# Column halves evicted from tiles of their own, weights loaded by K halves, attention rows dumped as they lie

## The chip, the core and the metric

The kernel runs on one core of one Trainium2 chip. A core has a matrix engine (TensorE; PE in the profile, with its weight loads shown as PEld), a vector engine (DVE), a scalar engine (ACT), GpSimd (POOL) and SyncE (SP), which here does nothing but issue transfers. Each engine works through its own list of instructions in order and waits on semaphores where it needs another engine's result. Sixteen DMA engines carry all transfers. A transfer that adds to what lies at its destination is issued by POOL; the plain ones are issued by SP, a few by ACT.

The metric is the device time of one execution in microseconds, the median of several runs.

## The reference

x has 2048 rows of 576 numbers in float32. The result is the sum of x, an attention and a two-layer network, both of the latter on the normalised rows.

```python
xn = _layernorm(x)
# attention: 32 heads of 18; each row looks at 8 rows: itself, 2 back, 4 back ... 14 back
qkv = (xn @ wqkv).reshape(B, S, 3, 32, 18)
idx = pos[:, None] - 2 * arange(8)[None, :]
logits = where(idx >= 0, einsum("bhsd,bhswd->bhsw", q, k[idx]) * 18 ** -0.5, -1e9)
A = einsum("bhsw,bhswd->bhsd", softmax(logits), v[idx]).reshape(B, S, 576) @ wo
# network: 576 -> 4608 -> 576
Bout = maximum(xn @ w1, 0) @ w2
out = x + A + Bout
```

## The kernel before, in words

**Precision.** Every operand of a matmul is split into a high and a low part in the type float32r, and three products (high times high, high times low, low times high) are added in PSUM. A split is two instructions, a copy on ACT (L172) and a subtraction on DVE (L176) or POOL (L174); `two` issues both.

**Stages.** The rows are cut into two phases of 1024 (even and odd rows). A phase has four blocks of 256 columns `tb` (each two row blocks of 128), and runs over the 36 blocks of 128 of the 4608 hidden columns. The first six blocks are multiplied plainly (`h_two`, `o_two`); the other thirty are taken in fifteen pairs p, two pairs of row blocks against two blocks of columns by Strassen's seven products. That makes 30 groups g in a phase; group g is for pair g // 2 of weights and pair g % 2 of `tb`. Each group is eight steps of TensorE, with places T and O in each step at which other work is issued. Between them run, for the four units u of eight heads, the qkv products; the attention itself (multiplications, reductions and softmax, all on DVE but the exponential) is a background list.

**What sets the order.** The program is written out in order by a planner: `on(ph, g, i, z, f, ...)` puts f at group g, step i, place T or O. The background list is issued by `run_bg`, which asks `room` how far DVE may run ahead of TensorE: up to the next of the due times DUE of a group (a step counts 1.46 us), 2.5 us at most. An instruction never moves at run time.

**Seeds.** A group keeps four banks of PSUM; `seed` (L977) opens bank q by copying bank a, and bank r by copying bank q, on ACT. The bank that is opened must have been read out before, by `relu_parts` (ACT L755, then DVE L759).

**Evictions.** The second matrix product leaves a block's 256 x 576 results in two PSUM tiles, columns 0 to 255 (h = 0) and 256 to 575 (h = 1). `evict` (L707) copies each half on ACT (L713) into one tile `ev` for both halves and both row blocks, of which there are two. When both halves are in, POOL issues two adding transfers to the output (L726), one for each row block, of 128 rows of 2304 bytes. In a group, the halves of one `tb` are evicted in steps 5 and 7, those of the other in steps 1 and 3 of the next group. The results of the output projection `wo` go out in the same way (L719), after the rows they add to have been added.

**Weights of the pairs.** `sw_load` (L894) brings four 256 x 128 pieces of w1 (two K halves for each of the two column blocks) in four transfers, and the 64 rows that are left over. `sw_mix` (L904) forms S1 to S4 of them on POOL (L909), `sw_prep` splits them.

**Attention rows.** `o_turn` turns a unit's result in blocks of 32 x 32 on DVE, `o_out` (L616) writes it to a DRAM tensor `od` in the order of the columns of the attention's result, by two transfers for each of four row groups r (L620 for 128 of the 144 columns, L624 for the other 16). When all units are there, `wo_rest` and `ot_in` bring the weights of `wo` and the rows of `od` back into SBUF (L257, L260; L395, L397), in five K tiles: four of 128 and one of 64, which is loaded twice.

## Time and profile before

| what | value |
|---|---|
| median of 3 runs | 1159.65 us (1159.57 to 1162.57) |
| profiled execution | 1158.69 us, span 1156.9 us, granted TensorE clock 0.994 |
| busy in the span: PE, DVE, ACT, POOL | 97%, 70%, 48%, 41% |
| DMA packets | 159811, 176.82 MB, 153 GB/s on average |
| adding transfers L726, POOL busy | 226.2 us |
| weight sums L909, POOL busy | 130.0 us, 120 of 1.1 us |
| subtractions L174, POOL busy | 95.8 us |
| seeds L977, ACT | 120 of 0.37 to 0.38 us |

Busy time counts what an engine executes, not what it waits for. A row of waits names the waiting engine, line and tile, then what released it, and the sum, number and longest of the waits. The chain of waits is followed back from the last instruction, so it shows what was late, not all that was slow. The time to landing of a transfer counts from its issue. PE's busy time comes near the whole span because matmuls overlap; the stalls have to be looked for in the waits.

### The profile page before, as it was taken

The page shows a single profiled execution, that of the slowest core. Times are in us where ns is not written, and L with a number is a line of the kernel's source. Part 1 is how long each engine was busy: PE and PEld are TensorE (multiplying, and loading weights), DVE is VectorE, ACT ScalarE, POOL GpSimd, SP SyncE. Part 2 cuts the span into 40 slices and gives each one's busy share as a digit, 9 for nine tenths or more (in the row PEclk, how much of TensorE's full clock was granted, in tenths as well). Part 3 has the DMA queues.
Part 4 walks back from the last instruction along what each step waited for, and adds up shares of the span by engine and source line. Part 5 has one row for each costly group of instructions (what it writes and reads, how often), then busy time and mean ns, then how long its engine had stood idle before and what let it go on. Part 6 is the DMA issues. An engine that isn't in the chain of part 4 may idle for free.

```text
span 1156.9 us, 38381 instructions
## 1 busy us (share of the span) xinstructions
PE 1116.8 (97%) x16410; PEld 1094.4 (95%) x16410; DVE 814.3 (70%) x1249; ACT 560.3 (48%) x1348; POOL 469.5 (41%) x514
## 2 busy tenths in 40 slices
PE   8999999999999999997999999999999999999896
PEld 8999999999999989997999999999999999999895
DVE  7676889699688677964317248868897896888521
ACT  4444464454454455564534345535545544555540
POOL 2324552453353345553322235435524523555331
PEclk9999999999999999998999999999999999999998
DMA  7469985795786687899947258759848957888984
GB/s 219 153 160 218 189 157 93 157 202 89 162 179 122 136 168 140 145 193 267 180 71 164 43 122 171 126 104 191 160 85 179 194 91 170 144 155 141 236 125 112
DMA packets 159811, 176.82 MB, mean 153 GB/s; under 512 B 36233, under 2 KB 107145, under 8 KB 159609
## 3 DMA queue, kind: packets, MB, share of 16 engines
q0 software_dynamic: 44352, 81.45, 46.8%
q1 hardware_dynamic: 114604, 92.03, 27.3%
q8 instruction: 129, 2.11, 0.7%
q10 hardware_dynamic: 684, 0.88, 0.2%
q14 instruction: 42, 0.34, 0.1%
HBM read 74.07 MB, written 95.70 MB: 147 GB/s over the span
## 4 chain that ended last, share of the span: by engine, by line
PE 74%; DMA 10%; DVE 5%; ACT 4%; issue 3%; POOL 1%; SPq 1%; ACTq 0%; DVEq 0%; POOLq 0%
PE po L163 23%; PE po L142 19%; PE ph L163 12%; PE pm L163 9%; PE pm L142 5%; DMA out<-ev 4%; PE ph L142 3%; DMA att<-od 2%; ACT ev L713 1%; PE ph L130 1%; DVE ar L759 1%; DVE ar L176 1%; PE po L130 1%; DVE wq L176 1%; DMA xS<-out 1%
## 5 line engine op out<-in xcount | busy, mean ns | idle before, releaser
L163 PE MATMUL po<-ar 64*128 64x320 f32 (+1 forms) x5760 | 469.2, 291 | 1.5 <-ACT ev L713 1.0
L163 PEld LDWEIGHTS po<-ar 64*128 64x128 f32 x5760 | 410.3, 185 | 4.1 <-ACT ev L713 1.6
L726 POOL DMA_DIRECT2D out<-ev x256 | 226.2, 1024 | 386.6 <-ACT ev L713 346.7
L163 PE MATMUL ph<-xT,ar 64*128 64x256 f32 x2520 | 323.5, 277 | 10.0 <-ACT pm L977 7.2
L163 PEld LDWEIGHTS ph<-xT,ar 64*128 64x128 f32 x2520 | 287.4, 185 | 15.5 <-ACT pm L977 10.3
L713 ACT ACTIVATE ev<-po 128x512 f32<-128x512 f32 (+1 forms) x266 | 171.5, 650 | 219.1 <-PE po L163 95.9
L163 PE MATMUL pm<-xS,ar 64*128 64x256 f32 x2160 | 261.1, 276 | 1.3 <-ACT u L981 0.6
L163 PEld LDWEIGHTS pm<-xS,ar 64*128 64x128 f32 x2160 | 236.9, 184 | 2.9 <-ACT u L981 1.3
L176 DVE TENSOR_TENSOR ar<-st,ar 128x256 fp32r<-128x256 f32 (+3 forms) x232 | 148.8, 646 | 87.5 <-ACT ar L172 76.4
L174 POOL TENSOR_TENSOR ar<-st,ar 128x256 fp32r<-128x256 f32 (+1 forms) x72 | 95.8, 1335 | 160.5 <-ACT ar L172 157.6
L172 ACT ACTIVATE ar<-st 128x256 fp32r<-128x256 f32 (+3 forms) x304 | 148.6, 503 | 15.2 <-DMA st<-in_w 11.5
L909 POOL TENSOR_TENSOR st<-st 128x256 f32<-128x256 f32 x120 | 130.0, 1096 | 12.1 <-DMA st<-in_w 7.7
L142 PE MATMUL po<-wq,xT 64*128 64x432 f32 x1296 | 134.0, 353 | 0.0
L142 PEld LDWEIGHTS po<-wq,xT 64*128 64x128 f32 x1296 | 120.2, 184 | 2.6
L163 PE MATMUL ph<-xS,ar 64*128 64x256 f32 x720 | 104.5, 278 | 9.5 <-ACT ph L977 9.1
L163 PEld LDWEIGHTS ph<-xS,ar 64*128 64x128 f32 x720 | 94.6, 186 | 12.6 <-ACT ph L977 11.8
L599 DVE TENSOR_TENSOR pr<-att 128x1152 f32<-128x1152 f32 x64 | 87.5, 1380 | 0.4
L564 DVE TENSOR_TENSOR pr<-att 128x1152 f32<-128x1152 f32 x64 | 86.4, 1351 | 0.2
L567 DVE TENSOR_REDUCE att<-pr 128x64 f32<-128x1152 f32 x64 | 85.2, 1339 | 0.0
L759 DVE SCALAR_TENSOR_TENSOR ar<-u,ar 128x256 fp32r<-128x256 f32 x60 | 29.8, 497 | 68.5 <-ACT ar L755 68.4
L606 DVE TENSOR_TENSOR pr<-pr 128x1152 f32<-128x1152 f32 x64 | 73.4, 1147 | 1.7
L142 PE MATMUL po<-ar 64*128 64x256 f32 (+1 forms) x984 | 71.0, 289 | 0.0
(121 smaller groups left out, 1360.8 us busy)
## 6 DMA issues: line engine op xcount, KB each, us to landing
out<-ev POOLq DMA_DIRECT2D x266, 288.0 KB, 6.0
st<-in_w SPq DMA_DIRECT2D x72, 288.0 KB
st<-in_w SPq DMA_DIRECT2D x120, 128.0 KB
att<-att SPq DMA_DIRECT2D x16, 441.0 KB
att<-in_wqkv SPq DMA_DIRECT2D x28, 216.0 KB
od<-att SPq DMA_DIRECT2D x32, 128.0 KB
att<-in_x SPq DMA_DIRECT2D x14, 288.0 KB
st<-in_w SPq DMA_DIRECT2D x60, 64.0 KB
```

The source lines that it names most:

```text
L142: ins = nc.tensor.matmul(o, l[z], r[z], start=start, stop=stop)
L163: b.ins = nc.tensor.matmul(b.ap, l[part], r[part], start=start, stop=stop, skip_group_check=skip)
L172: nc.scalar.activation(hi, src, AF.Copy)
L174: nc.gpsimd.tensor_tensor(lo, src, f32(hi), op=ALU.subtract)
L176: nc.vector.tensor_tensor(lo, src, f32(hi), op=ALU.subtract)
L564: nc.vector.tensor_tensor(pr[i], q, window(k, i), op=ALU.mult)
L567: nc.vector.tensor_reduce(lg[:, i], pr.pop(i).rearrange(heads, d=Dh), axis=AX.X, op=ALU.add)
L599: nc.vector.tensor_tensor(pr[i].rearrange(heads, d=Dh), e, window(v, i).rearrange(heads, d=Dh), op=ALU.mult)
L606: nc.vector.tensor_tensor(o, z[:, :, 0:n], z[:, :, n : 2 * n], op=ALU.add)
L713: nc.scalar.activation(acc[:, :, cols], z[:, :, 0 : cols.stop - cols.start], AF.Copy)
L726: ADDED[ph, 2 * tb + k] = nc.gpsimd.dma_start(o_v[ph, 2 * tb + k], acc[:, k, :], accum_op=ALU.add)
L909: nc.gpsimd.tensor_tensor(stg(o), stg(a), stg(b), op=op)
```

## The change

It has five parts.

1. `evict` takes a tile for each half (`ev0`, `ev1`, two of each) and issues the transfer right after the copy, one for both row blocks: 256 rows of 1024 or 1280 bytes. For `wo` blocks it issues two for each half. In the first phase's first third, where DVE adds x and SP writes plainly, the halves are handled in the same way.
2. The staging of the pair weights is laid out by K half: a row of the staging tile holds both column blocks, so `sw_load` needs two transfers for the four pieces, with rows of 1 KB. Sums and splits address it with a stride; S2 and A12 change places in the weight tile.
3. `od` holds each unit's 160 turned columns as they lie in SBUF (16 of them a second time), so that `o_out` is one transfer for each row group. `ot_in` picks 128 columns of each unit for the four large K tiles, and the last 16 of each unit for the fifth; `wo_load` picks the rows of `wo` in the same order.
4. The first split of a unit's qkv weights moves from step 3 to step 4.
5. The second due time of a group is 0.6 us earlier.

```diff
     def wo_load(ph, kt):
         if kt < KT:
-            nc.sync.dma_start(lo, wo2[kt * P : (kt + 1) * P, :])
+            nc.sync.dma_start(lo, wo2[kt * UD : kt * UD + P, :])
         else:
             for part in LOW, UPP:
-                nc.sync.dma_start(lo[part], wo2[KT * P : D, :])
+                nc.sync.dma_start(lo[part], wo2.rearrange("(u r) c -> u r c", u=NU)[:, P:UD])
...
         def o_out():
             for r in range(4):
-                nc.sync.dma_start(
-                    OD[ph][f : f + P, r].rearrange("(g j) t -> j g t", j=32),
-                    z[32 * r : 32 * r + 32, 0:4].rearrange("j g i e -> j g (i e)"),
-                )
-                nc.sync.dma_start(
-                    OD[ph][f + P : f + UD, r], z[32 * r + 16 : 32 * r + 32, 4].rearrange("j i e -> j (i e)")
-                )
+                nc.sync.dma_start(OD[ph][u, r].rearrange("g j t -> j g t"), z[32 * r : 32 * r + 32])
...
-        words_in(f32(lo), OD[ph][:, r])
+        z, od = f32(lo), OD[ph][:, r]
+        nc.sync.dma_start(z[:, 0:KT], od[:, 0:4].rearrange("u g j t -> (g j) u t"))
+        for part in LOW, UPP:
+            nc.sync.dma_start(z[part, KT], od[:, 4, 16:32])
...
+    def ev_tile(h):
+        return evp.tile([P, 2, CUT[h].stop - CUT[h].start], F32, name="ev%d" % h)
+
     def evict(ph, tb, h, z, what):
         cols = CUT[h]
-        nc.scalar.activation(acc[:, :, cols], z[:, :, 0 : cols.stop - cols.start], AF.Copy)
-        done.append(h)
-        if len(done) == 2:
-            del EV[key]
-            for k in range(2):
...
-                    ADDED[ph, 2 * tb + k] = nc.gpsimd.dma_start(o_v[ph, 2 * tb + k], acc[:, k, :], accum_op=ALU.add)
+        acc = EV[ph, tb, what][:, :, cols] if (ph, tb, what) in EV else ev_tile(h)
+        nc.scalar.activation(acc, z[:, :, 0 : cols.stop - cols.start], AF.Copy)
+        if what == "o":
+            ADDED[ph, tb, h] = nc.gpsimd.dma_start(
+                o_v[ph, 2 * tb : 2 * tb + 2, :, cols].rearrange("i p c -> p i c"), acc, accum_op=ALU.add
+            )
+            return
...
     def sw_load(ph, p):
-        for name, i, j in (("A11", 0, 0), ("S3", 1, 0), ("A22", 1, 1), ("A12", 0, 1)):
+        for j, r in enumerate((0, 2)):
             nc.sync.dma_start(
-                stg(name).rearrange("p (k c) -> p k c", k=2),
-                w1[2 * j * P : 2 * (j + 1) * P, f + i * P : f + (i + 1) * P].rearrange("(k p) c -> p k c", p=P),
+                ST[:, 512 * r : 512 * (r + 1)].rearrange("p (k c) -> p k c", k=2),
+                w1[2 * j * P : 2 * (j + 1) * P, f : f + 2 * P].rearrange("(k p) c -> p k c", p=P),
             )
...
-            for kt, (d, i) in enumerate(((-2, 3), (-2, 7), (-1, 1), (-1, 4), (-1, 6))):
+            for kt, (d, i) in enumerate(((-2, 4), (-2, 7), (-1, 1), (-1, 4), (-1, 6))):
...
-    DUE = (1.0, 3 * STEP + 1.6, 7 * STEP + 1.7, 8 * STEP + 1.0)
+    DUE = (1.0, 3 * STEP + 1.0, 7 * STEP + 1.7, 8 * STEP + 1.0)
```

TensorE's list is the same in both kernels. On DVE, in steps 3 to 6 of the group two before a unit's qkv products, the list before reads (`wq` is the split of the qkv weights, `att<-pr` a reduction of the attention, `ar<-pm` and `ar<-ph` the readings of PSUM banks behind which seeds wait):

```order
L564 TENSOR_TENSOR pr<-att 128x1152
L567 TENSOR_REDUCE att<-pr 128x64
L176 TENSOR_TENSOR ar<-st_2301,ar 128x320
L176 TENSOR_TENSOR wq<-att,wq 128x432
L759 SCALAR_TENSOR_TENSOR ar<-pm,ar 128x256
L176 TENSOR_TENSOR ar<-st,ar 128x256
L567 TENSOR_REDUCE att<-pr 128x64
L176 TENSOR_TENSOR ar<-st,ar 128x256
L759 SCALAR_TENSOR_TENSOR ar<-ph,ar 128x256
```

and now, at the same place on DVE:

```order
L564 TENSOR_TENSOR pr<-att 128x1152
L176 TENSOR_TENSOR ar<-st_2306,ar 128x320
L753 SCALAR_TENSOR_TENSOR ar<-pm,ar 128x256
L176 TENSOR_TENSOR ar<-st,ar 128x256
L176 TENSOR_TENSOR wq<-att,wq 128x432
L567 TENSOR_REDUCE att<-pr 128x64
L176 TENSOR_TENSOR ar<-st,ar 128x256
L753 SCALAR_TENSOR_TENSOR ar<-ph,ar 128x256
```

The reduction and the split of `wq` now stand behind the reading of bank `pm`, and one reduction fewer stands ahead of the reading of `ph`.

On POOL, from the last evictions of an even group of phase 0 through the odd group after it, the list before reads (L726 are the adding transfers, L909 the sums of weights, L174 low parts of the split of w2):

```order
L726 DMA out<-ev 128x576 x2
L909 TENSOR_TENSOR st<-st 128x256 x3
L726 DMA out<-ev 128x576 x2
L909 TENSOR_TENSOR st<-st 128x256
L726 DMA out<-ev 128x576 x2
L174 TENSOR_TENSOR ar<-st_2796,ar 128x256
L726 DMA out<-ev 128x576 x2
L174 TENSOR_TENSOR ar<-st_2796,ar 128x320
```

and now, at the same place on POOL:

```order
L711 DMA out<-ev_2602 128x2x320
L905 TENSOR_TENSOR st<-st 128x2x128
L711 DMA out<-ev_2662 128x2x256
L905 TENSOR_TENSOR st<-st 128x2x128 x2
L711 DMA out<-ev_2729 128x2x320
L905 TENSOR_TENSOR st<-st 128x2x128
L711 DMA out<-ev_2797 128x2x256
L711 DMA out<-ev_2864 128x2x320
L711 DMA out<-ev_2925 128x2x256
L174 TENSOR_TENSOR ar<-st_2802,ar 128x256
L711 DMA out<-ev_2997 128x2x320
L174 TENSOR_TENSOR ar<-st_2802,ar 128x320
```

The transfer of the first half now stands ahead of the two sums, or of the low part, behind which the pair stood before; the transfer of the second half keeps the pair's place.

On SP, at the end of phase 0, from the last of four such pairs of `od` transfers on, the list before reads:

```order
L620 DMA od<-att 32x4x256
L624 DMA od<-att 16x256
L207 DMA st_9861<-in_w 128x576
L257 DMA att<-wo_143 128x576 x2
L260 DMA att<-wo_143 64x576 x2
L207 DMA st_9898<-in_w 128x576
L395 DMA att<-od 128x4x256
L397 DMA att<-od 64x256 x2
```

and now, with all four `od` transfers in the first row:

```order
L619 DMA od<-att 32x5x256 x4
L207 DMA st_9876<-in_w 128x576
L257 DMA att<-wo_143 128x576 x2
L260 DMA att<-wo_143 64x1x576 x2
L207 DMA st_9913<-in_w 128x576
L661 DMA att<-od 128x4x256
L663 DMA att<-od 64x1x256 x2
```

Eight issues have become four, and the 64 rows that are left over come from four places of 16 rows (64x1x576).

More of the change, by code (lines that the diff above doesn't have):

```diff
@@ L813, in tile_body @@
     PB = [None] * 4
+    XO = {}
     def o_two(n):
@@ L1299, in last_group @@
         for j in range(2):
[L1300 removed]
+            EV[ph, 2 * (g % 2) + j, "o"] = z[:, 1 - j]
         for j in (0, 2):
@@ L1424, in tile_body @@
         late(b + 18, sw_prep, ph, 0, "A11", "S1")
-        late(b + 20, sw_prep, ph, 0, "S2", "A12")
+        late(b + 20, sw_prep, ph, 0, "A12", "S2")
         late(b + 22, sw_prep, ph, 0, "S3", "S4")
```

75 lines of the change are left out of this document (34 added, 41 removed).

## The prediction

> **What bounds the kernel now.** I read the page first, then the list of waits, TensorE's part of it before all others, then the chain of waits and the timelines at the stalls.
>
> ```profile
> PE 1116.8 (97%) x16410; PEld 1094.4 (95%) x16410; DVE 814.3 (70%) x1249; ACT 560.3 (48%) x1348; POOL 469.5 (41%) x514
> ```
>
> TensorE (PE) is busy for 1116.8 of 1156.9 us. The change leaves its instructions and their order alone, so all that can be won or lost is PE's idle time, and what PE waits for tells what may be won. In the list of waits, with the total, the number of times and the longest in us:
>
> ```profile
> PE ph L163 <- ACT ph L977: 9.1, 6, 3.8
> PE ph L163 <- ACT pm L977: 7.2, 12, 0.9
> PE ph L142 <- ACT xT L422: 2.2, 1, 2.2
> PE ph L163 <- ACT ar L172: 1.2, 1, 1.2
> PE po L163 <- ACT ev L713: 1.0, 3, 0.4
> ```
>
> L977 is the seeding copy (PSUM to PSUM, on ScalarE, "ACT") that opens a Strassen bank. It is 0.38 us long, so what makes it late is in front of it. For the first row that is ScalarE itself, held at an eviction (L713) whose buffer has not been emptied:
>
> ```profile
> ACT ev L713 <- DMA out<-ev: 54.5, 20, 3.8
> ```
>
> The chain of waits shows one such case near the end (start, length, what):
>
> ```profile
> 1085.64 0.44 POOL out L726
> 1086.08 0.14 issue
> 1086.22 8.39 DMA out<-ev
> 1094.61 0.02 issue
> 1094.63 0.04 ACTq L713
> 1094.67 0.05 issue
> 1094.72 0.60 ACT ev L713
> ...
> 1096.85 0.28 ACT ph L977
> ```
>
> The adding transfer of the second row block, issued at 1086.22, lands 8.39 us later; the eviction then runs, and four instructions behind it L977, for which PE stands still. For the second row it is VectorE (DVE) that is late, in its timeline:
>
> ```profile
> 145.93 1.34 DVE L567 TENSOR_REDUCE att<-pr 128x64 f32<-128x1152 f32 x1
> 147.19 0.55 DVE L176 TENSOR_TENSOR ar<-st,ar 128x320 fp32r<-128x320 f32 x1
> 147.66 1.13 DVE L176 TENSOR_TENSOR wq<-att,wq 128x432 fp32r<-128x432 f32 x1
> 148.71 0.41 DVE L759 SCALAR_TENSOR_TENSOR ar<-pm,ar 128x256 fp32r<-128x256 f32 x1
> ```
>
> L759 reads the old bank, L977 may only then overwrite it, and PE restarts at 149.64 after 0.89 us:
>
> ```profile
> 149.64 0.38 PE L163 MATMUL ph<-xT,ar 64*128 64x256 f32 x1 [0.89 <-ACT pm L977]
> ```
>
> Such a stall stands before each of the three later attention units of both phases: six of the twelve.
>
> **The change part by part.** *Weight split and due time.* The first `wq_split` of a unit moves from step 3 to step 4 and the due time DUE[1] comes 0.6 us earlier, so that TENSOR_REDUCE (1.34) and the wq split (1.13) go behind L759 pm. That bank is free 2.4 us sooner, more than the longest stall (0.9), and the next deadline on DVE (L759 ph) has one reduce fewer ahead of it than before. Two further stalls of 0.6 us, before `wo_split`, lose their reduce too. What is late next is the attention itself, whose steps end later, by a step or so; its consumer is one group away, except at the end of a phase (below). I take 6.2 of the 7.2 us and leave the four short stalls.
>
> *Evictions.* Before, a buffer of both halves was taken at the first half (step 1) and sent only after the second (step 3), as two transfers issued one behind the other. Now each half has two buffers of its own and is sent when it is written. The wait in the row of 54.5 us stands only at the first half's eviction; there the transfer is issued two steps (2.9 us by the planner's 1.46) earlier and is alone instead of second. In every second group it stands on POOL (GpSimd) behind the first weight sum (L909), which waits for its loads; then little is won, but nothing lost, since the second half no longer holds the buffer. A wait of at most 3.8 us goes by that; the second half's buffer is needed two steps later than the first's, so it has at least as much time as it had. So the first row's 9.1 us go as far as evictions cause them: 5.3 us outside the end of phase 0, whose 3.8 us I count below. Of the last row 0.7 us go with them.
>
> *What the evictions cost.* The number of adding transfers stays 264 (and the six `wo` blocks that add get four each instead of two), but each row of 2304 bytes becomes two, of 1024 and 1280 bytes. POOL first, by the line's own view (shortest, median, longest in ns):
>
> ```profile
> L726 POOL DMA_DIRECT2D out<-ev x256: 592/897/1224, 79.7 to 1110.7; - x128
> POOL out L726 <- ACT ev L713: 346.7, 82, 14.0
> ```
>
> With 256 rows instead of 128 an issue costs between 0.9 us (nothing more) and 1.8 us (all of it per row). At worst POOL's 470 us grow by 264 x 0.9 = 238 to 708, 61% of the span, and it waits 347 us for evictions as it is. I take nothing on PE. The DMA engines are the dearer side:
>
> ```profile
> q0 software_dynamic: 44352, 81.45, 46.8%
> q1 hardware_dynamic: 114604, 92.03, 27.3%
> q8 instruction: 129, 2.11, 0.7%
> ```
>
> Queue 0 is the adding one: 46.8% of 16 x 1156.9 us over some 35,300 rows (81.4 MB of 2304 B) is 245 ns a row, 106 ns/KB. Queue 1 pays 5053 us for 92.03 MB, 55 ns/KB, with packets of 803 B on average; queue 8's 16 KB packets pay about 61 ns/KB, so a fixed part per packet can't be read from that pair. Bounds for splitting a row: nothing (all by bytes) and twice the time (all per packet). The nearest row is queue 1, where a packet of 803 B costs 44 ns in all; so that bounds what a packet can cost beside its bytes. I take a third of it, 14 ns, as fixed, and twice that for an adding row, which reads both sides: 28 ns or 11% of a row, an estimate nearer to the lower end because a whole plain packet of nearly this size costs less than a fifth of an adding row. The Trainium skill, "DMA: Bandwidth & Descriptors", section "Why small descriptors are slow (HBM only)", gives some 3 cycles a packet; at its 850 MHz that is an estimate of 7 ns a row, 3%, and the sum would be 2.5 us less. No run here shows it yet.
>
> *Weights by K halves.* 120 transfers of 128 KB with rows of 512 B become 60 of 256 KB with rows of 1 KB: 15,360 packets and 60 issues fewer. L909's first sum now waits for a load that also brings A12: 128 KB, 0.9 us at the 149 GB/s of the window 800 to 860 (below). Behind it on POOL stand that group's evictions, which have the time just won. Nothing on PE.
>
> *Attention rows, and the two ends of phases.* There the DMA engines are full (columns: window, length, then busy time of PE, its loads, DVE, ACT, POOL; clock, DMA share, GB/s):
>
> ```profile
> 490.00:545.00 55.00, 48.62 (x743) 47.30 (x739) 29.46 (x52) 29.22 (x70) 24.00 (x27) 0.97 1.00 219
> 800.00:860.00 60.00, 59.18 (x871) 58.44 (x869) 54.76 (x75) 29.74 (x72) 26.52 (x29) 1.00 0.77 149
> ```
>
> and the chain at the end of phase 0 runs through the first window:
>
> ```profile
> 507.81 2.97 DMA od<-att
> ...
> 511.30 6.56 DMA att<-wo
> ...
> 517.87 11.75 DMA att<-od
> ...
> 530.15 7.22 DMA att<-od
> ...
> 537.39 5.67 DMA xT<-words
> ```
>
> The last lands at 543.06, and PE goes on at 544.29 with phase 1. A stall taken away just ahead (3.8 us) is no gain here: this chain sets the start. Its change has three parts. (a) Eight issues of od become four:
>
> ```profile
> L620 SPq DMA_DIRECT2D od<-att x32: 337/420/1407, 203.4 to 1075.5; - x32
> L624 SPq DMA_DIRECT2D od<-att x32: 370/443/2024, 203.9 to 1076.0; - x32
> ```
>
> The four L624 and part of the long ones go, some 3.2 of 5.1 us, but o_turn stands three DVE instructions (1.4 us) later: 1.8 us earlier in all. (b) The table again, for L726 alone (busy time on POOL, count; clock, DMA share, GB/s), at the ends of phase 0 and 1:
>
> ```profile
> 490.00:545.00 55.00, 14.14 (x16) 0.97 1.00 219
> 1062.00:1100.00 38.00, 10.63 (x12) 1.00 1.00 218
> ```
>
> 16 adding transfers of 128 rows at 245 ns on 16 engines are 31 us of DMA time; 11% of that is 3.4 us. (c) The remainder rows of `wo2` and of od are now taken out of four units, 16 rows each (64x1x576 where it was 64x576). The trace has one such shape, the adding transfer L719 to 4 x 32 rows, beside L726 with the same bytes to 128 rows:
>
> ```profile
> DMA to landing us min/median/max: 4.0/5.9/9.9
> ...
> DMA to landing us min/median/max: 10.2/11.2/14.4
> ```
>
> It lands 5.3 us later. A plain transfer costs half an adding one per KB (55 to 106), so 2.65 us for 288 KB: 2.65 for the wo remainder and 1.2 for that of each od block, of which the chain passes two: 5.0 at most, nothing at least (if other engines' work hides it); I take 3. The Trainium skill has this as a rule ("DMA: Bandwidth & Descriptors", "Why a DMA increments its semaphore by 16 and not by 1"): a transfer uses as many of the 16 engines as divide the outer sizes of both sides, here 4. The two landings agree with it. Sum of the end of phase 0: -1.8 + 3.4 + 3 = +4.6 us.
>
> At the end of phase 1 the same o_out holds a w2 load, and PE stalls 1.2 us for it (fourth row, 0.3 with its split):
>
> ```profile
> 1071.22 5.75 DMA od<-att
> ...
> 1077.04 6.76 DMA st<-in_w
> ```
>
> The issue 1.8 us earlier takes that away: -1.3 us (with a little left). The last 10 us after PE's end stay.
>
> *Sum.* -6.2 - 5.3 - 0.7 - 1.3 + 4.6, and +1 for short stalls that the new DVE order may open: -7.9 us. The profiled execution took 1158.69 us (span 1156.9); that gives 1150.8, and the median of the runs, 1159.65, stands 0.96 above: **1152 us**, 0.7% faster. A measurement of this kernel tells 0.3%, 3.5 us, from no change.
>
> **The rivals.** *Adding rows are dear (slower).* If a half row costs nearly a whole one, queue 0 rises with factor p. The end of phase 0 alone pays 31 x (p - 1) us, against 13.5 us of gains less 2.2 us (parts a and c, and the 1 us): from p = 1.36 on it is no gain, and at p = 1.6, with half of the same at the end of phase 1 (12 transfers, 23.5 us) it is 1159.65 - 11.3 + 18.6 + 7 = 1174. At p = 2 queue 0 would need 94% and all queues over 120% of the span, some 1400 us. For it: the DMA share of 1.00 at both ends. Against: 44 ns for a whole packet of 803 B in queue 1.
>
> *Narrow loads decide (about the same).* All 5.0 us of (c), again at the end of phase 1 before the `wo` blocks, and half the gains refilled by other stalls: -6.8 + 6.6 + 3, some 1162.
>
> *Full gain.* The shorter adding packets let the loads pass between them, and the end of phase 0 loses nothing or gains 2 us: -13.5 - 2 + 1, 1145; with all of the five rows gone, 1139.
>
> *The transfers do not go earlier,* since POOL's queue holds them: only DVE's 6.2 and the 1.3 us are won, against 4.6: 1157.
>
> **How the numbers follow.** My forecast (1147 to 1156) 0.50; full gain 0.20; narrow loads 0.12; dear rows 0.14; held by POOL 0.04. The likeliest gives 1152. The range leaves out most of the dear rows and the far end of the full gain: 1140 to 1166. Faster by over 0.3%: 0.50 + 0.20 = 0.70; slower: 0.14 and half of the narrow loads, 0.20; within: the other half and held by POOL, 0.10.
>
> **What would show it.** Right: the row ACT ev L713 <- DMA (its new line) under 10 us, the six stalls of 0.9 us gone, PE's rows on L977 under 5 us together; queue 0 near 52% with some 79,000 packets; PE's idle time between 490 and 550 up by about 5 us. Wrong: queue 0 over 60%, or DMA waits at the second half's eviction, or L909 waiting for its loads, with PE waiting on weights behind it.

## The result: slower, where a gain was forecast

The changed kernel takes 1168.86 us (median, 1163.63 to 1170.91), the kernel before 1160.94 in the same series (1156.96 to 1162.57): a ratio of 1.0056 with a 95% interval of 1.0036 to 1.0075. The forecast was 1152 us, 1140 to 1166. Its profiled execution took 1169.23 us with a span of 1167.5, against 1158.69 and 1156.9 before; 10.6 us are to be explained. The times in the table of experiments are medians, too, without one execution of `cut_retune` that took 6260 us.

In the changed kernel some lines have other numbers: the eviction is L709 (before L713), its adding transfer L711 (L726), the seed L973 (L977), DVE's reading of a bank L753 (L759), the weight sum L905 (L909), the split of od's rows L670 (L674), od's transfers L619 (L620, L624), its loads L661 and L663 (L395, L397).

First the page of the kernel after, the engines and the two large DMA queues (queue, packets, MB, share of 16 engines):

```profile
PE 1123.6 (96%) x16410; PEld 1101.6 (94%) x16410; DVE 857.5 (73%) x1249; ACT 563.9 (48%) x1348; POOL 567.9 (49%) x526
...
q0 software_dynamic: 84480, 81.49, 51.6%
q1 hardware_dynamic: 102908, 92.55, 27.5%
```

PE does the same 16410 matmuls as before and is busy 6.8 us longer with them (1123.6 against 1116.8); its idle time in the span goes from 40.1 to 43.9 us. So most of the loss is not in waits at all: part of the matmuls ran slower. The list of waits of the kernel after, PE's part and ACT's waits for transfers:

```profile
PE ph L163 <- ACT ph L973: 10.9, 2, 6.1
PE ph L163 <- ACT ar L172: 4.1, 2, 2.3
PE ph L163 <- ACT pm L973: 4.0, 9, 0.7
PE po L142 <- ACT ev L709: 2.5, 3, 2.0
...
ACT ar L172 <- DMA st<-in_w: 23.4, 10, 7.6
ACT att L670 <- DMA st<-in_w: 6.9, 1, 6.9
ACT att L670 <- DMA att<-od: 5.5, 1, 5.5
```

The row of 54.5 us of evictions waiting for their buffers is gone, and the row on `pm` has fallen from 7.2 to 4.0 us. But the first row, 9.1 us in six waits before, is now 10.9 us in two, and ACT waits for transfers elsewhere: for weights (L172), and for od or a weight load in front of the split of od's rows (L670).

Where in the program it happens is read from the same four seeds in both kernels, the 1st, 55th, 61st and 113th of 120. In the timeline of ACT (start, length), before:

```profile
111.15 0.36 ACT L977 ACTIVATE ph<-ph 128x256 f32<-128x256 f32 x1
499.02 0.37 ACT L977 ACTIVATE ph<-ph 128x256 f32<-128x256 f32 x1
680.77 0.36 ACT L977 ACTIVATE ph<-ph 128x256 f32<-128x256 f32 x1
1055.61 0.37 ACT L977 ACTIVATE ph<-ph 128x256 f32<-128x256 f32 x1
```

and after:

```profile
110.81 0.36 ACT L973 ACTIVATE ph<-ph 128x256 f32<-128x256 f32 x1
496.18 0.37 ACT L973 ACTIVATE ph<-ph 128x256 f32<-128x256 f32 x1
685.49 0.37 ACT L973 ACTIVATE ph<-ph 128x256 f32<-128x256 f32 x1
1058.39 0.37 ACT L973 ACTIVATE ph<-ph 128x256 f32<-128x256 f32 x1
```

| stage | before, us | after, us | difference | the prediction's terms |
|---|---|---|---|---|
| groups of phase 0 (to the 55th seed) | 387.9 | 385.4 | -2.5 | with phase 1: -8.4 (-6.2, -2.5 of the evictions' 5.3, -0.7, +1) |
| end of phase 0, plain start of phase 1 (to the 61st) | 181.7 | 189.3 | +7.6 | +4.6 |
| groups of phase 1 (to the 113th) | 374.8 | 372.9 | -1.9 | see the first row |
| end of phase 1 (to the span's end) | 101.3 | 109.1 | +7.8 | -4.1 (-1.3, and the stall of 2.8 us put down to an eviction) |

The groups won 4.4 us. Both ends lost 15.4.

**Why the matmuls are slower.** The views by windows of the kernel after, at the end of phase 0 (window, length, then busy us of PE, its loads, DVE, ACT, POOL; granted clock, DMA share, GB/s):

```profile
513.30:516.70 3.40, 1.33 (x16) 1.13 (x18) 1.23 (x2) 2.10 (x6) 1.55 (x2) 1.00 0.99 271
516.70:520.10 3.40, 3.40 (x32) 3.40 (x32) 1.18 (x2) 2.05 (x6) 2.37 (x3) 0.50 1.09 234
520.10:523.50 3.40, 3.40 (x62) 3.40 (x61) 1.92 (x4) 2.13 (x4) 1.20 (x1) 0.99 1.15 275
```

PE stands still for 2.1 us of the first window, the clock is granted at one half for the whole of the next, and 32 matmuls get through where 62 do in the one after. A stall of 1.8 us (the wait for L172 that ends at 515.03) thus costs some 1.7 us more. After the stalls at 515, 532, 567, 1089 and 1105 us the kernel after has 23.9 us at half clock, the kernel before 6.8 us, after its stalls at 528 and 544. That is 17 us more at half speed, 8.5 us of work, of which PE's busy time shows 6.8, since PE stands still in part of that time. In the kernel before, the stall of 2.77 us at 1097 cost none; its windows:

```profile
1092.20:1095.60 3.40, 2.21 (x33) 1.97 (x29) 0.58 (x2) 0.88 (x3) 0.00 (x0) 1.00 1.10 253
1095.60:1099.00 3.40, 1.82 (x30) 1.82 (x32) 2.90 (x7) 3.40 (x10) 0.96 (x2) 1.00 1.10 286
1099.00:1102.40 3.40, 3.40 (x59) 3.40 (x58) 2.38 (x5) 2.16 (x6) 0.79 (x1) 1.00 1.09 197
```

The half-clock stretches of a trace lie on a fixed grid of 3.41 us; here the stall falls on two windows of it, 1.2 and 1.6 us idle, and the clock stays.

### The profile page after: what moved, and what is told of

The parts are those of the page before. It is cut to its first block, busy times and chain, and to the rows that moved or that the text cites. A ratio compares the mean times of both kernels' runs of the same rounds, so it can differ in the third digit from the quotient of the medians.

```text
span 1167.5 us, 38294 instructions
## 1 busy us (share of the span) xinstructions
PE 1123.6 (96%) x16410; PEld 1101.6 (94%) x16410; DVE 857.5 (73%) x1249; ACT 563.9 (48%) x1348; POOL 567.9 (49%) x526
## 3 DMA queue, kind: packets, MB, share of 16 engines
q0 software_dynamic: 84480, 81.49, 51.6%
## 4 chain that ended last, share of the span: by engine, by line
PE 78%; DMA 7%; DVE 7%; ACT 2%; issue 2%; SPq 2%; DVEq 0%; ACTq 0%; POOL 0%
PE po L163 25%; PE po L142 20%; PE ph L163 13%; PE pm L163 10%; PE pm L142 4%; DMA st<-in_w 4%; PE ph L142 3%; DVE ar L753 2%; DVE pr L564 1%; DVE ar L176 1%; PE ph L130 1%; DMA att<-od 1%; PE po L130 1%; ACT ev L709 1%; DMA xS<-od 1%
## 5 line engine op out<-in xcount | busy, mean ns | idle before, releaser
L711 POOL DMA_DIRECT2D out<-ev x256 | 305.1, 1212 | 386.5 <-ACT ev L709 174.7
L163 PEld LDWEIGHTS po<-ar 64*128 64x128 f32 x5760 | 404.5, 186 | 5.6 <-ACT ev L709 1.9
L163 PE MATMUL ph<-xT,ar 64*128 64x256 f32 x2520 | 326.9, 279 | 10.7 <-ACT ar L172 4.1
L709 ACT ACTIVATE ev<-po 128x512 f32<-128x512 f32 (+1 forms) x266 | 171.6, 650 | 205.7 <-PE po L163 128.2
L176 DVE TENSOR_TENSOR ar<-st,ar 128x256 fp32r<-128x256 f32 (+3 forms) x232 | 157.9, 685 | 78.4 <-ACT ar L172 67.3
L172 ACT ACTIVATE ar<-st 128x256 fp32r<-128x256 f32 (+3 forms) x304 | 148.6, 503 | 28.1 <-DMA st<-in_w 23.4
L174 POOL TENSOR_TENSOR ar<-st,ar 128x256 fp32r<-128x256 f32 (+1 forms) x72 | 98.4, 1375 | 87.5 <-ACT ar L172 86.7
L905 POOL TENSOR_TENSOR st<-st 128x256 f32<-128x256 f32 x120 | 131.0, 1109 | 13.0 <-DVE ar L176 6.7
L163 PE MATMUL ph<-xS,ar 64*128 64x256 f32 x720 | 105.6, 281 | 11.1 <-ACT ph L973 10.9
L163 PEld LDWEIGHTS ph<-xS,ar 64*128 64x128 f32 x720 | 97.1, 189 | 12.2 <-ACT ph L973 11.4
L564 DVE TENSOR_TENSOR pr<-att 128x1152 f32<-128x1152 f32 x64 | 93.6, 1463 | 0.2
L599 DVE TENSOR_TENSOR pr<-att 128x1152 f32<-128x1152 f32 x64 | 89.8, 1418 | 0.7
L606 DVE TENSOR_TENSOR pr<-pr 128x1152 f32<-128x1152 f32 x64 | 79.6, 1243 | 1.4
L142 PEld LDWEIGHTS po<-ar 64*128 64x128 f32 x984 | 67.2, 187 | 2.6 <-ACT ev L709 2.4
```

The costliest lines, as they stand in the source:

```text
L142: ins = nc.tensor.matmul(o, l[z], r[z], start=start, stop=stop)
L163: b.ins = nc.tensor.matmul(b.ap, l[part], r[part], start=start, stop=stop, skip_group_check=skip)
L172: nc.scalar.activation(hi, src, AF.Copy)
L174: nc.gpsimd.tensor_tensor(lo, src, f32(hi), op=ALU.subtract)
L176: nc.vector.tensor_tensor(lo, src, f32(hi), op=ALU.subtract)
L564: nc.vector.tensor_tensor(pr[i], q, window(k, i), op=ALU.mult)
```

## The experiments

Every run below computes all that the kernels compute. Each was timed against the kernel before on the same chip; what counts is the ratio with its 95% interval. Before the first runs there were three theories: (1) the transfers at the two ends, dearer through cut rows and narrow loads; (2) the attention itself, made late by the new due time; (3) the cut adding rows alone.

| run | what it is | us | ratio to before |
|---|---|---|---|
| no_dump | changed, part 3 undone | 1162.74 | 1.0014 (1.0000 to 1.0027) |
| no_cut | changed, part 1 undone | 1166.36 | 1.0032 (1.0014 to 1.0050) |
| retune | before with parts 4 and 5 | 1158.27 | 0.9974 (0.9956 to 0.9993) |
| no_due | changed, part 5 undone | 1170.07 | 1.0068 (1.0052 to 1.0084) |
| wide_od | changed, od's remainder in one piece | 1169.00 | 1.0046 (1.0025 to 1.0067) |
| wide_wo | changed, wo's remainder in one piece | 1160.99 | 0.9979 (0.9965 to 0.9992) |
| cut_retune | before with parts 1, 4, 5 | 1161.84 | 0.9993 (0.9971 to 1.0015) |
| khalf_retune | before with parts 2, 4, 5 | 1156.84 | 0.9945 (0.9926 to 0.9964) |
| no_cut_wide | changed, part 1 undone, wo's remainder in one piece | 1158.16 | 0.9965 (0.9947 to 0.9983) |
| cut_mix | wide_wo with POOL's second sum one place earlier | 1160.75 | 0.9984 (0.9967 to 1.0001) |
| khalf | before with part 2 | 1161.19 | 0.9993 (0.9972 to 1.0013) |
| cut | before with part 1 | 1164.43 | 1.0010 (0.9996 to 1.0024) |
| rows_cut | khalf_retune with the adding rows cut | 1178.54 | 1.0150 (1.0119 to 1.0180) |
| pair | khalf_retune with one adding transfer for both row blocks | 1154.31 | 0.9943 (0.9921 to 0.9965) |

### Which part loses

**Part 3 undone.** od's eight issues and row order, and wo2's loads, as before:

```diff
...
-                nc.sync.dma_start(OD[ph][u, r].rearrange("g j t -> j g t"), z[32 * r : 32 * r + 32])
+                nc.sync.dma_start(OD[ph][f : f + P, r].rearrange("(g j) t -> j g t", j=32), ...)
+                nc.sync.dma_start(OD[ph][f + P : f + UD, r], ...)
...
-                nc.sync.dma_start(lo[part], wo2.rearrange("(u r) c -> u r c", u=NU)[:, P:UD])
+                nc.sync.dma_start(lo[part], wo2[KT * P : D, :])
...
```

> The changed kernel with its third part undone: od and wo2 are written and read as before the change (rows of wo in their order, remainder of 64 rows in one piece), all else as changed. Theory 1 (the two phase ends are full of transfers; what the change adds there, cut adding rows and remainders taken out of four places, makes the loads land later, and each stall of PE of about 2 us costs a window of 3.4 us at half clock besides): the remainders are wide again, so the 6.1 and 4.8 us stalls behind L670 shrink by 2 to 4 us each and the second half-clock window behind each of them goes; 1159 to 1164 us. Theory 2 (what is late is the attention itself, by the new due time, and all behind it): nothing here moves the due time, so 1167 to 1170 us, as the changed kernel. Theory 3 (the cut adding rows alone fill the windows): 1166 to 1170 us, and eight issues of od instead of four on SP even make it 1 or 2 us worse.

Measured 1162.74: theory 1's range. Three quarters of the loss (0.42 of 0.56%) go with the attention rows.

**Part 1 undone** (`evict`, `o_out` and what depends on them as before):

```diff
...
-            ADDED[ph, tb, h] = nc.gpsimd.dma_start(
-                o_v[ph, 2 * tb : 2 * tb + 2, :, cols].rearrange("i p c -> p i c"), acc, accum_op=ALU.add
+                    ADDED[ph, 2 * tb + k] = nc.gpsimd.dma_start(o_v[ph, 2 * tb + k], acc[:, k, :], accum_op=ALU.add)
...
```

> The changed kernel with its first part undone: one tile for both halves, two adding transfers of 128 rows of 2304 bytes, all else as changed. The evictions then wait for their buffers again (54.5 us of ACT, some 5 us of PE). Theory 1: half of the loss at the phase ends goes with the cut rows, the waits for buffers come back: 1164 to 1168 us. Theory 2 (attention late by the due time): the ends stay as they are and the 5 us of waits come on top, 1170 to 1175 us. Theory 3 (the cut adding rows alone): the stalls at both ends go back to those of before (3.8 and 2.8 us) and so do the half-clock windows, while the gain of the DVE order stays: 1154 to 1160 us.

Measured 1166.36, again theory 1's range; theory 3 falls. With the rows whole, the two stalls at the ends are even longer, as its waits show:

```profile
PE ph L163 <- ACT ph L976: 22.1, 7, 9.5
...
ACT att L670 <- DMA att<-od: 18.4, 2, 9.2
```

**The two planner numbers alone:**

```diff
-            for kt, (d, i) in enumerate(((-2, 3), (-2, 7), (-1, 1), (-1, 4), (-1, 6))):
+            for kt, (d, i) in enumerate(((-2, 4), (-2, 7), (-1, 1), (-1, 4), (-1, 6))):
...
-    DUE = (1.0, 3 * STEP + 1.6, 7 * STEP + 1.7, 8 * STEP + 1.0)
+    DUE = (1.0, 3 * STEP + 1.0, 7 * STEP + 1.7, 8 * STEP + 1.0)
```

> The kernel before with the fourth and fifth part alone (first split of the qkv weights one step later, second due time 0.6 us earlier). The prediction's first term stands here by itself: 6.2 us of PE's waits go. Theories 1 and 3: 1152 to 1156 us, the phase ends as before. Theory 2 (the later attention makes the ends late): the six stalls of 0.9 us go, but w2's load behind the later od transfers holds PE at the end of phase 1 for 2 us or more with a half-clock window behind it: 1158 to 1163 us.

Measured 1158.27, 3 us won where the prediction's term was 6.2; inside what theory 2 expected, not 1 and 3. Its waits:

```profile
PE ph L163 <- ACT ph L977: 12.8, 7, 6.8
PE ph L163 <- ACT pm L977: 0.7, 3, 0.2
...
ACT att L674 <- DMA att<-od: 10.7, 3, 7.5
```

The row on `pm` falls from 7.2 to 0.7 us, all that was forecast. Of that, a part is given back at the ends: by the seeds, its groups are 4.0 and 2.6 us shorter, its ends 0.6 and 3.5 us longer. PE comes to the split of od's rows earlier, od does not come as much earlier, and ACT waits 7.5 us for it.

**The due time undone** in the changed kernel:

```diff
-    DUE = (1.0, 3 * STEP + 1.0, 7 * STEP + 1.7, 8 * STEP + 1.0)
+    DUE = (1.0, 3 * STEP + 1.6, 7 * STEP + 1.7, 8 * STEP + 1.0)
```

> The changed kernel with the second due time back at its old value, all else as changed. Theory 2: od goes out earlier at both ends, the w2 load behind it too, the stalls at L172 and half of those at L670 go: 1157 to 1162 us. Theories 1 and 3: the transfers are as many and as narrow as before this edit, 1166 to 1170 us, and some 3 us of the six stalls before the later attention units may be back.

Measured 1170.07. The due time is not what loses; theory 2 falls as the main cause.

### Which load of part 3

**od's remainder in one piece:**

```diff
-                nc.sync.dma_start(OD[ph][u, r].rearrange("g j t -> j g t"), z[32 * r : 32 * r + 32])
+                nc.sync.dma_start(OD[ph][0][u, r].rearrange("g j t -> j g t"), z[32 * r : 32 * r + 32, 0:4])
+                nc.sync.dma_start(OD[ph][1][r, 16 * u : 16 * u + 16], z[32 * r + 16 : 32 * r + 32, 4])
...
-            nc.sync.dma_start(z[part, KT], od[:, 4, 16:32])
+            nc.sync.dma_start(z[part, KT], OD[ph][1][r])
```

> The changed kernel, but the 16 left-over columns of each unit go to a place of their own in DRAM by a second transfer for each row group (eight issues of od again), so that the two remainder loads of each od block are 64 rows in one piece; the remainder of wo stays taken out of four places. Theory 1a (the od remainders decide: they lie in the chain itself, and the run without the second-half cut shows SP held 6.35 us at one of their issues): the stalls behind L670 at both ends shrink to about 3 us with one half-clock window each, 1162 to 1165 us. Theory 1b (the wo remainder decides, being 288 of the 416 narrow KB at its place and first in the queue): no more than 1.5 us gained, 1167 to 1170 us. Theory 1c (it is neither the shape but that eight issues became four): as the run with the third part undone, 1162 to 1164 us, in both this run and none in the next.

**wo's remainder in one piece:**

```diff
-            nc.sync.dma_start(lo, wo2[kt * UD : kt * UD + P, :])
+            nc.sync.dma_start(lo, wo2[kt * P : (kt + 1) * P, :])
...
-                nc.sync.dma_start(lo[part], wo2.rearrange("(u r) c -> u r c", u=NU)[:, P:UD])
+                nc.sync.dma_start(lo[part], wo2[KT * P : D, :])
...
-            at(b + 12, nc.sync.dma_start, wo2, wo)
+            by_unit = wo.rearrange("(u r) c -> u r c", u=NU)
+            at(b + 12, nc.sync.dma_start, wo2[0 : KT * P, :].rearrange("(u r) c -> u r c", u=NU), by_unit[:, 0:P])
+            at(b + 12, nc.sync.dma_start, wo2[KT * P : D, :].rearrange("(u r) c -> u r c", u=NU), by_unit[:, P:UD])
```

> The changed kernel, but wo2 in DRAM has its left-over rows together at its end (written so by two copies early in the first phase), so that its remainder loads are 64 rows in one piece; the od remainders stay taken out of four places. Theory 1a: at most 1.5 us gained, 1167 to 1170 us. Theory 1b: 1162 to 1165 us. Theory 1c: no gain, 1168 to 1170 us.

I had favoured the od remainders (1a), since they stand in the chain. Measured: 1169.00 with od wide, which puts back the four issues that part 3 had saved, and 1160.99 with wo wide. It is the two remainder loads of wo, 288 KB, taken out of four places of 16 rows instead of 64 rows in one piece (1b). The same bytes in one piece save 0.77% of the time, 8.9 us, more than the whole loss of 0.56%; and without the cut evictions they save 0.67% (no_cut against no_cut_wide). With wo wide the rest of part 3 is a gain: 0.9979, against 1.0014 without part 3. What they do is seen in the run without the cut evictions (`no_cut`), while PE stands still behind the split of od's rows (columns as above):

```profile
518.00:520.00 2.00, 0.00 (x0) 0.00 (x0) 0.00 (x0) 0.00 (x0) 0.00 (x0) 1.00 0.79 154
520.00:522.00 2.00, 0.00 (x0) 0.00 (x0) 0.00 (x0) 0.00 (x0) 0.00 (x0) 0.69 0.47 127
522.00:524.00 2.00, 0.00 (x0) 0.00 (x0) 0.00 (x0) 0.06 (x1) 0.00 (x0) 0.50 0.48 155
```

No engine works, and from 520 us on the DMA engines are loaded to half only, as if all waited for a few of them. In the kernel after it is the same, less sharply:

```profile
526.00:528.00 2.00, 0.23 (x3) 0.00 (x0) 0.00 (x0) 0.00 (x0) 0.00 (x0) 1.00 0.72 175
528.00:530.00 2.00, 0.00 (x0) 0.00 (x0) 0.00 (x0) 0.74 (x2) 0.00 (x0) 1.00 0.68 207
```

The run without the cut evictions and with wo wide (`no_cut_wide`, below) has a stall of 8.2 us at the same place, but with the DMA engines full while no engine works:

```profile
524.00:526.00 2.00, 0.00 (x0) 0.00 (x0) 0.00 (x0) 0.00 (x0) 0.00 (x0) 1.00 1.06 219
526.00:528.00 2.00, 0.00 (x0) 0.00 (x0) 0.00 (x0) 0.00 (x0) 0.00 (x0) 0.89 0.95 235
```

The od loads stand behind those of wo, and SP is held while it issues them. The issue of one od remainder at the end of phase 0 (shortest, median, longest in ns), without the cut evictions:

```profile
L663 SPq DMA_DIRECT2D att<-od x4: 520/562/6350, 507.5 to 518.8; - x4
```

and the same with wo wide:

```profile
L663 SPq DMA_DIRECT2D att<-od x4: 537/576/2841, 513.2 to 517.9; - x4
```

With the cut evictions the longest falls from 2604 to 1035 ns.

By the same four seeds, wo wide takes 5.1 us off the end of phase 0 (189.3 to 184.2) and 3.7 off the end of phase 1 (109.1 to 105.4), while the groups stay within 0.4. A stall of 5.1 us is left at the end of phase 0, at 536.65, after the split of od's rows.

From od's first issue to the start of its split the kernel after takes 25.5 us at the end of phase 0 (503.8 to 529.3) and 24.6 at the end of phase 1 (1077.5 to 1102.1); with wo wide 19.2 and 18.6, in the kernel before 20.1 and 19.3. By itself this span does not price the loads: with part 3 undone it is 23.9 and 20.3, and in `no_cut_wide` 24.9 and 21.9. The Trainium skill's rule on how many of the 16 engines a transfer uses ("DMA: Bandwidth & Descriptors", "Why a DMA increments its semaphore by 16 and not by 1") gives four for these loads and 16 for 64 rows in one piece; the half-loaded windows agree with it.

### The other parts alone

**Parts 1, 4 and 5, and parts 2, 4 and 5 on the kernel before** (hunks as in the change):

> The kernel before with the first part (evictions by halves) and the fourth and fifth part (the two planner numbers); weights and attention rows as before. If the parts add up (the runs so far give -3.4 us for the two numbers, +6.1 for the attention rows, +2.5 for the evictions in the presence of the attention rows, +2 left for the weights): 1160 to 1162 us, and no wait of an eviction for its buffer. If the cut rows cost only because they meet the narrow loads: 1152 to 1156 us, since the 5 us of eviction waits go as well.

> The kernel before with the second part (weights laid out by K halves) and the two planner numbers alone. If the weights' part is harmless, as the prediction had it: 1157 to 1159 us, as the two numbers alone. If the parts add up: 1160 to 1161 us, with POOL's sums waiting for their loads, or DVE's splits later.

**Part 2 alone, and part 1 alone:**

> The kernel before with the second part alone (weights laid out by K halves). The prediction had nothing on PE for it. Two runs differ by 3 us for it in the presence of the two planner numbers. If that is real: 1157 to 1159 us; if it is the scatter between chips and runs: 1160 to 1163 us.

> The kernel before with the first part alone (evictions by halves). The prediction: 5.3 us of eviction waits on PE go, the cut rows cost 3.4 us at the end of the first phase, 1157 to 1159 us. By the runs so far (the evictions cost 2 to 8 us wherever they were added): 1163 to 1169 us, with ACT's waits for eviction buffers gone all the same.

Measured 1161.84, 1156.84, 1161.19 and 1164.43: the first as the sum of the parts had it, the second with part 2 harmless, the third at the scatter, the fourth as the runs before it had it. Part 2 costs nothing (0.9993 alone), as the prediction had it; what it gains beside the planner numbers (0.9945 against 0.9974) is within their intervals, and with part 1 there it points the other way (cut_retune 0.9993, no_dump 1.0014). Part 1 wins nothing: 1.0010 alone, 0.1 to 0.2% lost in three pairs that differ by it alone (retune and cut_retune, no_cut and the changed kernel, no_cut_wide and wide_wo), and 0.7% between khalf_retune and no_dump. So the parts do not simply add up. Its waits, alone:

```profile
PE ph L163 <- ACT pm L974: 9.6, 17, 0.9
ACT att L674 <- DMA att<-od: 9.0, 2, 5.5
PE ph L163 <- ACT ph L974: 7.6, 2, 4.8
```

No eviction waits for a buffer any more. But the two long stalls are still there, 4.8 and 2.8 us, now with od behind them, and the row on `pm`, for which DVE is late, has grown from 7.2 to 9.6 us. One reason for DVE is in its groups (count, busy us, mean ns), before:

```profile
L759 DVE SCALAR_TENSOR_TENSOR ar<-m,ar 128x256 fp32r<-128x256 f32 x60 | 32.1, 535 | 2.0 <-ACT ar L755 2.0
```

and with part 1 alone:

```profile
L757 DVE SCALAR_TENSOR_TENSOR ar<-m,ar 128x256 fp32r<-128x256 f32 x60 | 62.1, 1035 | 2.3 <-ACT ar L753 2.0
```

The timeline of the kernel after shows the reading of m in two groups, in one of which POOL has no sum to do:

```profile
727.63 1.22 POOL L711 DMA_DIRECT2D out<-ev  x1 [1.42 <-ACT ar L749]
...
728.01 0.42 DVE L753 SCALAR_TENSOR_TENSOR ar<-m,ar 128x256 fp32r<-128x256 f32 x1
...
739.30 1.20 POOL L711 DMA_DIRECT2D out<-ev  x1 [0.64 <-ACT ar L749]
739.34 0.42 DVE L753 SCALAR_TENSOR_TENSOR ar<-u,ar 128x256 fp32r<-128x256 f32 x1 [0.68 <-ACT ar L749]
739.69 1.88 DVE L753 SCALAR_TENSOR_TENSOR ar<-m,ar 128x256 fp32r<-128x256 f32 x1
740.09 2.09 POOL L905 TENSOR_TENSOR st<-st 128x256 f32<-128x256 f32 x2
```

Beside the issue of a transfer alone the reading takes 0.42 us; where a sum now stands behind that issue and runs against it, 1.88.

**POOL's sum one place earlier,** with DVE's list the same, on wide_wo:

```diff
-                on(ph, a - 1, 1, "O", sw_mix, 1)
+                on(ph, a - 1, 1, "T", sw_mix, 1)
```

> The changed kernel with wo's remainder together in DRAM, and with POOL's second weight sum put ahead of the eviction's adding transfer instead of behind it (one place earlier in step 1; DVE's list stays the same). Theory 4 (the cut evictions cost through DVE: the sum now stands behind the first half's transfer on POOL and runs against DVE's reading of m, which goes from 0.46 to 1.0 us on average, DVE's work grows by 32 us and the attention comes 2 us later): DVE's busy time falls from 857 to under 835 us and the time to 1156 to 1159 us. Theory 5 (they cost through the DMA engines, 84,000 packets instead of 44,000 ahead of the loads at the ends): DVE's time may fall, the time stays at 1160 to 1162 us.

Measured 1160.75, no gain on wide_wo, as theory 5 has it. DVE's work fell only from 857.5 to 846.1 us and the mean of DVE's reading of m from 991 to 897 ns, so the collision was moved more than removed, and the run speaks against theory 4 less than its time suggests.

**Rows cut, all else of part 1 left away,** on khalf_retune:

```diff
-                    ADDED[ph, 2 * tb + k] = nc.gpsimd.dma_start(o_v[ph, 2 * tb + k], acc[:, k, :], accum_op=ALU.add)
+                    c = CUT[k]
+                    ins = nc.gpsimd.dma_start(
+                        o_v[ph, 2 * tb : 2 * tb + 2, :, c].rearrange("i p c -> p i c"), acc[:, :, c], accum_op=ALU.add
+                    )
...
```

> The kernel before with the weights laid out by K halves and the two planner numbers (1156.8 us), and in it only the rows of the adding transfers cut: both halves still go into one tile and are sent after the second half, but as two transfers of 256 rows of 1024 and 1280 bytes instead of two of 128 rows of 2304. The waits of evictions for their buffers stay. Theory 5 (the cut rows themselves cost, in the DMA engines and in POOL's longer issues): 1160 to 1164 us, as with the whole first part (1162.7). Theory 4 (the price is the place of the transfers: each half sent at once, ahead of POOL's sums, which then run against DVE): no loss, 1156 to 1158 us, and DVE's work near 821 us.

**One transfer of whole rows for both row blocks,** on khalf_retune:

```diff
-                    ADDED[ph, 2 * tb + k] = nc.gpsimd.dma_start(o_v[ph, 2 * tb + k], acc[:, k, :], accum_op=ALU.add)
+                    if k == 0:
+                        ins = nc.gpsimd.dma_start(
+                            o_v[ph, 2 * tb : 2 * tb + 2].rearrange("i p c -> p i c"), acc, accum_op=ALU.add
+                        )
+                    ADDED[ph, 2 * tb + k] = ins
```

> The same base, with one adding transfer for both row blocks instead of two, the rows whole (256 rows of 2304 bytes), sent after the second half. Theory 5: no loss, 1155 to 1158 us, since POOL issues half as many transfers and the packets are as before; if POOL's issue is paid by the row, one issue takes as long as two did. Theory 4: the same, 1155 to 1158 us. If it is slower by 3 us or more, it is neither the cut nor the place but the bundling of both row blocks, whose buffer is then free only when all 256 rows have landed.

Measured 1178.54 and 1154.31: bundling is free, cutting the rows costs 2%, more than theory 5 expected. DVE's work is 829 us with the rows cut, so theory 4 does not explain this loss. The adding line's view on POOL with the rows cut (shortest, median, longest in ns):

```profile
L728 POOL DMA_DIRECT2D out<-ev x256: 757/1203/1812, 79.1 to 1135.1; - x128
...
DMA to landing us min/median/max: 4.1/6.4/11.3
```

and with whole rows, both row blocks in one:

```profile
L727 POOL DMA_DIRECT2D out<-ev x128: 767/1203/1430, 79.6 to 1106.5; - x128
...
DMA to landing us min/median/max: 5.7/7.1/10.5
```

An issue of 256 rows takes 1203 ns at the median, whatever their length, where one of 128 took 897. Cut rows need two such issues where whole rows need one of them or two shorter ones, and POOL's work goes from 473 to 556 us (pair: 401.5). The buffer is free only when the second has landed:

```profile
ACT ev L713 <- DMA out<-ev: 78.3, 23, 5.2
```

where khalf_retune has

```profile
ACT ev L713 <- DMA out<-ev: 71.5, 31, 3.9
```

The loss lies in the groups (by the seeds 11.1 and 9.2 us more than khalf_retune). ACT waits little more in all, but longer at a time: behind waits of 4.3 to 5.2 us stand four stalls of PE of 1.0 to 1.5 us, where khalf_retune has none above 0.7 in the groups. These make up 5.3 us; the rest is spread over shorter stalls and was not traced. How much of it is POOL's and how much the DMA engines' was not separated. The whole of part 1, with tiles of its own for each half and its transfer sent at once, wins most of it back: no_dump, the same but for that, is at 1.0014.

**Part 1 undone and wo wide** (both edits above):

> The changed kernel with wo's remainder together in DRAM (64 rows in one piece) and the first part undone (whole rows evicted from one tile, two adding transfers of 128 rows of 2304 bytes). If the narrow remainder of wo was what made the attention rows dear, and the evictions cost on top of it: the stalls of 9.5 and 8.9 us that the run without the cut evictions had at the two ends shrink to 3 or 4 us, and the time is 1152 to 1157 us, below both kernels, with the 50 to 70 us of eviction waits on ACT still there and harmless. If the cut evictions save what the prediction said (5.3 us): no better than the run with the wide remainder alone, 1160 to 1164 us.

Measured 1158.16, 7.8 us below the same with wo narrow, below both kernels, though a little above what was expected. The stalls do not show the gain: its two are still 8.2 and 4.7 us long and its evictions wait 57.5 us, but the profiled execution, 1164.53 us, is the slowest of its twelve. The best of all, khalf_retune and pair, leave out parts 1 and 3: 0.55% below the kernel before.

## Why the prediction was wrong, point by point

- **"-1.3 us" at the end of phase 1 is the step that failed,** with the 2.8 us beside it that was put down to an eviction: that stage went from 101.3 to 109.1 us where 4.1 us less was forecast, 12 of the 18.5 us by which the sum was off. Of the 7.8 us by which it grew, 3.6 are idle time of PE, and 4.2 are busy time, with the matmuls at half clock behind the stalls. Two things were wrong. The price of the narrow loads was put on the end of phase 0 alone, though the same loads run at the end of phase 1, where wo wide takes 3.7 us off. And od did not go out 1.8 us earlier, at either end: its first issue stands 19.1 us behind the 113th seed where it stood 15.6 (1077.51 and 1071.22), which the issues saved only just make up, since its last one stands 20.5 us behind it where it stood 20.4. (The planner numbers alone put the first issue at 16.9, part 1 alone at 17.9.) The load of w2 behind od goes out at 1079.40, 21.0 us behind the seed instead of 21.4, but lands after 8.8 us instead of 6.8, and its stall grew from 1.2 to 2.3 us. Why it lands later was not separated: with part 1 undone it takes 6.8 us again, with wo wide 9.4.
- **The narrow loads, "2.65 for the wo remainder",** were the right mechanism with too small a size: I took 3 us for all narrow loads together, and wo's alone are worth 5.1 and 3.7 us at the two ends by the seeds, 8.9 us of the time by the run. The price had come from the landing of one adding transfer of that shape against a wide one; here both loads of 144 KB stand in a full queue, beside the adding transfers and with od behind them. "At most 5.0" was no bound, and od's own remainder, for which I had taken 1.2 each, costs nothing measurable beside the four more issues that its run needs. The rival that had these loads decide came nearest, and had them at 6.6 us in all.
- **A stall was priced at its length.** Its half-clock window was left out: PE's busy time grew by 6.8 us. The page of before showed it at a clock of 0.97 in the window from 490 to 545 us, quoted and not used.
- **"-5.3 us" for the evictions did not come.** ACT's 54.5 us did go. But 2.8 of the 5.3 us stood at the end of phase 1, where od holds the same split and takes over, and against the rest stands a later DVE (row on `pm` 9.6 instead of 7.2 us, alone).
- **"-6.2 us" for the DVE order** was right by the row, which falls to 0.7 us in the run with that alone, and the run is 3 us faster: PE was no longer late there, and so earlier at the next bound, which had not moved.
- **The cut rows at 11%** were right: queue 0 was forecast near 52% and some 79,000 packets, and is at 51.6% and 84,480; 976 us more over 40,128 more packets are 24 ns each (28 forecast). The end of phase 0 was forecast 4.6 us longer and was 7.6. That the same rows cost 2% where one tile takes both halves (rows_cut) was not seen.
- **Of what was to be seen,** the row of evictions is gone, and so, by their place in PE's list, are all six stalls of 0.9 us. But three stalls of 0.66 us on `pm` have opened at other matmuls of phase 1 (at 791.50, 884.75 and 978.06); part 1 alone has them too, the planner numbers alone do not. The two stalls of 0.6 us before `wo_split` are still there, with 0.67 and 0.42. PE's rows on L973 are at 14.9 us and not under 5, for the reason above. PE's idle time between 490 and 550 rose by 2.4 us (6.4 to 8.8) and not by 5; over the whole end of phase 0 it rose by 4.5 us, and PE's busy time, at half clock, by 3.0.
- **POOL's longer issues were taken at nothing on PE** because POOL waits 347 us for evictions. That cover holds for POOL's share of time, not for the instruction just behind the issue: it moved a sum against DVE. What that cost stays open, since the run that moved the sum back did so only in part.

## What to carry to other kernels

A stage that ends on a full DMA queue sets its own start: gains ahead of it can come back as a wait there, so price a change first at such ends, for every time the end occurs. There, the shape of a load counts more than its bytes: 64 rows in one piece instead of four places of 16 was worth 0.8% of this kernel. And a stall of PE of about 2 us can cost nearly twice its length, where it falls into one window of the clock and the next one runs at half.

## What the runs showed of the hardware

- **The clock goes by how much of a fixed 3.41 us window PE was idle.** In the traces of fifteen kernels of this case, among full-clock windows of the grid behind the first 60 us, none with up to 1.50 us idle was followed by one at half clock, each with 1.80 us or more was, and of the seventeen between (1.52 to 1.78) four were. The Trainium skill's "TensorE: Matmul & The Clock Gate" has the free-running window of 3413 ns ("Part 1: The HAM clock gate (the "warmup" mystery)"), and the traces agree; its rule against idle gaps of more than some 3.4 us ("HAM oscillation — how this bites in real kernels") is too kind here: a window with 2.1 us idle, 1.8 of it in one gap, is enough, and a gap of 2.77 us across two is not.
- **A POOL issue of an adding transfer has a fixed and a row part.** The medians of 897 ns for 128 rows and 1203 for 256 give, if the cost grows evenly with the rows, some 2.4 ns a row and 0.6 us fixed; the 256 rows took the same with 1, 1.3 or 2.3 KB each; so half as many issues of twice the rows took POOL from 473 to 401.5 us of work at the same time of the kernel.
- **A DVE operation of 0.42 us can take 1.88 us beside POOL's sums,** 60 of them 1.0 us on average instead of 0.54. The Trainium skill ("SBUF — State Buffer", "SBUF: two separate sides") has a DVE operation with two inputs in SBUF and a GpSimd operation that reads SBUF take turns on one pair of ports, each for its whole length; the timeline agrees, with the sum and not with the issue beside it.
